# A warm-up of wide and thin matrix products in place of 22 transposes, ahead of a fused attention and MLP kernel

## The chip, the cores and the metric

The kernel runs on one core of a Trainium2 chip. The metric is device time in microseconds (us). Beside the two timed runs there is one profiled execution, whose span (first to last instruction) is 913.8 us.

## The reference

```python
def _A_ref(x, wqkv, wo):                       # x: 1 x 2048 x 640, 32 heads of 20, window of 256
    qkv = (x @ wqkv).reshape(B, S, 3, H, Dh).transpose(2, 0, 3, 1, 4)
    q, k, v = qkv[0], qkv[1], qkv[2]
    scores = einsum("bhqd,bhkd->bhqk", q, k) * Dh ** -0.5
    scores = where(mask, scores, -1e9)         # causal, 256 keys back
    o = einsum("bhqk,bhkd->bhqd", softmax(scores), v)
    return o.transpose(0, 2, 1, 3).reshape(B, S, D) @ wo

def _B_ref(x, w1, b1, w2, b2):                 # 640 -> 1536 -> 640
    h = relu(x @ w1 + b1)
    return (h * h) @ w2 + b2

xn = layernorm(x)
return x + _A_ref(xn, wqkv, wo) * silu(_B_ref(xn, w1, b1, w2, b2))
```

All inputs and the output are fp32. Nothing of the warm-up enters the output.

## The kernel before

Every fp32 matrix is split into a high part rounded to fp32r and a low part, and a product is taken as three fp32r products (high by high, high by low, low by high). The attention's inner products use bf16 and fp16 pieces in the same way.

The first stage normalizes x in four blocks of 512 rows, transposes them on TensorE, and computes q, k (first group of 128 columns) and v. The second stage walks over 16 pairs of heads by 16 blocks of 128 queries, and between its steps a filler feeds TensorE with the remaining q and k groups, the MLP's two layers and at last the output projection.

In the first stage the order of work on all five engines is the order in which the code writes it (`manual_schedule`). It begins like this. ScalarE loads its table (line 275). TensorE runs the warm-up: `WARM` = 22 transposes of an identity matrix into one PSUM tile (line 278), which wait only for GpSimd to make the identity. Meanwhile SyncE issues the loads of the first four tiles of x (`load_x`, line 134) and of the weights for k and q (`load_w`, line 174) and v (line 298). VectorE takes the statistics of x (`stats`, lines 142 and 143), ScalarE the root (line 302), VectorE the reciprocal and the normalized rows `xn` (lines 305 and 151). TensorE transposes `xn` in five pieces of 128x128 (line 311), runs ten more transposes of the identity (line 325, `WARM2`), and goes on with the next tile. ScalarE and VectorE take the high and low parts out of PSUM (lines 317 and 321). The first products of q and k are at line 200, those of v at line 230. Line 578 is the helper through which most wide products of the second stage go, line 527 the product of the attention's weights with v (61 columns), lines 448 and 492 the scores, lines 464, 465 and 474 a row of maxima that is transposed on TensorE.

The pools: `bigp` has eight buffers of 128 x 2560 four-byte elements, used for x transposed and large weights; `pat` has two PSUM buffers under each of the tags "s" and "st"; `pmm` has three.

The lines of the warm-up:

```python
warm_ps = pmm.tile([P, P], F32, tag="mm", name="warm_ps")
for _ in range(WARM):
    nc.tensor.transpose(warm_ps, ident, ident)
```

Of the kernel before, what the change touches and what calls it, by code (L numbers as in the profile page):

```python
# [7 lines left out]
F32 = mybir.dt.float32  # L8
F32R = mybir.dt.float32r
BF16 = mybir.dt.bfloat16  # L10
# [4 lines left out]
P = 128  # L15
# [23 lines left out]
WARM = 22  # L39
# [12 lines left out]
def attn_mlp_kernel(ctx: ExitStack, tc, x, wqkv, wo, w1, b1, w2, b2, out):  # L52
    nc = tc.nc
    PSUM = bass.MemoryType.PSUM
    const = ctx.enter_context(tc.tile_pool(name="const", bufs=1))
    bigp = ctx.enter_context(tc.tile_pool(name="bigp", bufs=8))
    pmm = ctx.enter_context(tc.tile_pool(name="pmm", bufs=3, space=PSUM))
    pat = ctx.enter_context(tc.tile_pool(name="pat", bufs=2, space=PSUM))
# [21 lines left out]
    ident = const.tile([P, P], F32, name="ident")  # L80
# [46 lines left out]
    with tc.tile_pool(name="ph1v", bufs=2) as p1v, tc.tile_pool(name="ph1", bufs=2) as p1, tc.tile_pool(name="ph1x", bufs=4) as p1b, tc.tile_pool(name="ph1w", bufs=1) as p1w:  # L127
# [145 lines left out]
        with tc.manual_schedule(engines={E_.PE, E_.Activation, E_.DVE, E_.Pool, E_.SP}):  # L273
            warm = p1.tile([P, 1], F32, tag="warm", name="warm")
            nc.scalar.activation(warm, eps, AF.Sqrt)
            warm_ps = pmm.tile([P, P], F32, tag="mm", name="warm_ps")
            for _ in range(WARM):
                nc.tensor.transpose(warm_ps, ident, ident)
            ws0, ws1 = {}, {}
            load_x(0, 3)  # L280
            raws = [load_w(group_src(0, "k"), KC)]
# [159 lines left out]
    def scores(p, q, between):  # L441
        i = p % 2
        k0 = max(0, q - 2)
        nk = (q - k0 + 1) * P
        r = []
        for hh in range(2):
            ps = pat.tile([P, 4 * P], F32, tag="s", name="sps")
            nc.tensor.matmul(ps[:, :nk], qs[i][0:KR, hh, q * P:(q + 1) * P], ks[i][0:KR, hh, k0 * P:k0 * P + nk], start=True, stop=True)  # L448
            r.append(ps)
            if not hh:  # L450
                rows = between and between(ps)
        return (r, nk), rows
# [547 lines left out]
    with tc.manual_schedule(engines={E_.PE, E_.Activation, E_.DVE, E_.Pool, E_.SP}):  # L1000
# [6 lines left out]
        for s in range(steps):  # L1007
# [17 lines left out]
            rows = between = None  # L1025
            if s % 4 == 0 and 0 < s <= NP * NT:
                def between(tp=None, s=s):
                    return max_rows((s - 1) // NT, (s - 1) % NT // 4, tp)
            if a:
                sc, rows = scores(p, q, between)  # L1030
            elif between:
                rows = between()
# [58 lines left out]
```

## Time and profile before

| what | value |
|---|---|
| time, median of two runs | 915.86 us (915.09 to 916.62) |
| span of the profiled execution | 913.8 us |
| TensorE products, busy | 893.6 us, 98% |
| TensorE weight loads, busy | 746.9 us, 82% |
| VectorE, busy | 759.1 us, 83% |
| ScalarE, busy | 668.6 us, 73% |
| GpSimd, busy | 544.9 us, 60% |
| mean granted TensorE clock | 0.998 |

The profile names engines PE (TensorE products), PEld (its weight loads), DVE (VectorE), ACT (ScalarE), POOL (GpSimd) and SP (SyncE). A timeline row gives the start in us, the time in us from the first start to the last end of the instructions merged into it, the engine, the line of the code, the operation with output and inputs, and how many there are; in brackets stands the idle time before it and what ended it. A row of a group gives busy time and the mean duration of one in ns. The records of a matrix product overlap, since products are pipelined, so a record is longer than the distance from one product to the next.

### The profile page before, as it was taken

To read this page: it belongs to the slowest core of one execution; us is meant where nothing else is said; L and a number is where in the kernel's file an instruction comes from. 1 tells how busy PE (TensorE), PEld (TensorE's weight loads), DVE (VectorE), ACT (ScalarE), POOL (GpSimd) and SP (SyncE) were. 2 spreads that over 40 slices of the span, in tenths; PEclk is the share of its full clock that TensorE was granted. 3 is DMA by queue.
4 is the path that set the end of the run, shared out by engine and by line. 5 is a ranking of instruction groups with operands and counts; after the bars stand their busy time and mean duration, and the time that the engine had idled before them with its cause. 6 is when DMAs were issued, how large, how long until landed. Compare 5 with 4: busy or idle time off the path is not lost.

```text
span 913.8 us, 21792 instructions
## 1 busy us (share of the span) xinstructions
PE 893.6 (98%) x7632; PEld 746.9 (82%) x7632; DVE 759.1 (83%) x2031; ACT 668.6 (73%) x1282; POOL 544.9 (60%) x832
## 2 busy tenths in 40 slices
PE   8999999999999999999999999999999999999998
PEld 8999977776766678788788788778788788789998
DVE  7875478999899998998888999998988988975554
ACT  5454348898889896987886988976986977994321
POOL 6010017797789785886785876775775976772000
PEclk9999999999999999999999999999999999999999
DMA  6899786767777454244264245365174264156873
GB/s 240 279 394 350 219 266 201 233 209 237 250 237 237 142 180 131 89 155 132 67 203 152 69 123 153 103 224 152 51 262 136 75 211 145 27 158 222 286 272 117
DMA packets 130803, 168.79 MB, mean 185 GB/s; under 512 B 44100, under 2 KB 91268, under 8 KB 128132
## 3 DMA queue, kind: packets, MB, share of 16 engines
q1 hardware_dynamic: 130692, 167.39, 56.3%
q8 instruction: 60, 0.98, 0.4%
q14 instruction: 51, 0.42, 0.1%
HBM read 96.15 MB, written 70.91 MB: 183 GB/s over the span
## 4 chain that ended last, share of the span: by engine, by line
PE 73%; DVE 9%; ACT 8%; DMA 4%; issue 3%; POOL 2%; SPq 1%; ACTq 0%; DVEq 0%; POOLq 0%
PE yps L872 14%; PE hps L578 14%; PE wops L578 8%; PE sps L448 7%; PE qkps L578 7%; PE ops L527 7%; PE stps L492 6%; PE vps L230 5%; ACT p L499 3%; DVE junk L460 2%; PE qkps L200 2%; DVE pl L513 2%; ACT ph L507 1%; DMA v_d<-vt 1%; ACT relu L827 1%
## 5 line engine op out<-in xcount | busy, mean ns | idle before, releaser
L499 ACT ACTIVATE p<-stps,ebias 128x384 f32<-128x384 f32 (+2 forms) x512 | 258.7, 558 | 85.2 <-PE stps L492 72.9
L460 DVE CUSTOM_DVE_ANT_0 junk<-sps,mask 128x384 bf16<-128x384 f32 (+2 forms) x512 | 250.5, 525 | 47.3 <-PE sps L448 40.8
L513 DVE TENSOR_TENSOR pl<-p,ph 128x768 f16<-128x768 f32 (+2 forms) x256 | 251.3, 982 | 1.9 <-ACT ph L507 1.9
L500 POOL TENSOR_SCALAR_AFFINE_SELECT p<-p 128x256 f32<-128x256 f32 x256 | 166.9, 652 | 128.4 <-ACT p L499 112.0
L507 ACT ACTIVATE ph<-p 128x768 f16<-128x768 f32 (+2 forms) x256 | 204.6, 799 | 4.1 <-POOL p L502 3.0
L872 PE MATMUL yps<-w,hh 128*128 128x320 f32 x768 | 183.8, 320 | 0.0
L578 PE MATMUL hps<-xb,w 128*128 128x512 f32 x630 | 172.1, 410 | 0.0
L578 PEld LDWEIGHTS hps<-xb,w 128*128 128x128 f32 x630 | 115.3, 188 | 24.1
L872 PEld LDWEIGHTS yps<-w,hh 128*128 128x128 f32 x768 | 130.7, 188 | 5.0 <-issue 0.6
L448 PE MATMUL sps<-ks,qs 120*128 120x384 bf16 (+2 forms) x512 | 128.2, 319 | 4.5 <-DVE mt L460 4.4
L872 PE MATMUL yps<-w,hl 128*128 128x320 f32 x384 | 122.5, 319 | 0.0
L492 PE MATMUL stps<-qs,ks 122*128 122x384 bf16 (+2 forms) x512 | 120.8, 316 | 1.2 <-DMA qs<-mrow 1.0
L502 POOL TENSOR_SCALAR_AFFINE_SELECT p<-p 128x256 f32<-128x256 f32 x224 | 109.0, 487 | 0.0
L527 PEld LDWEIGHTS <-ph 128*128 128x128 f16 x1440 | 85.9, 97 | 25.6 <-issue 20.6
L527 PE MATMUL ops<-vp,ph 128*128 128x61 bf16 x1440 | 100.9, 192 | 0.0
L527 PE MATMUL ops<-vp,pl 128*128 128x61 bf16 x1440 | 99.7, 191 | 0.0
L831 POOL TENSOR_TENSOR hl<-sq,hh 128x256 fp32r<-128x256 f32 x96 | 77.5, 808 | 18.9 <-DVE sq L830 15.6
L527 PEld LDWEIGHTS <-pl 128*128 128x128 f16 x1440 | 87.7, 97 | 0.0
L872 PEld LDWEIGHTS yps<-w,hl 128*128 128x128 f32 x384 | 72.2, 188 | 1.5
L492 PEld LDWEIGHTS <-ks 122*128 122x128 bf16 x512 | 49.0, 98 | 29.5 <-issue 2.5
L230 PE MATMUL vps<-wv,xT 128*128 128x320 f32 x480 | 71.7, 308 | 0.2 <-DVE r L255 0.2
L230 PEld LDWEIGHTS vps<-wv,xT 128*128 128x128 f32 x480 | 70.5, 188 | 0.6 <-DVE r L255 0.5
(116 smaller groups left out, 1480.3 us busy)
## 6 DMA issues: line engine op xcount, KB each, us to landing
ks<-k_d SPq DMA_DIRECT2D x64, 240.0 KB
qs<-q_d SPq DMA_DIRECT2D x64, 240.0 KB
xb<-xs SPq DMA_DIRECT2D x12, 1280.0 KB
xs<-xT SPq DMA_DIRECT2D x8, 1280.0 KB
y<-ysb SPq DMA_DIRECT2D x32, 320.0 KB
q_d<-shm SPq DMA_DIRECT2D x38, 256.0 KB
v_d<-vt SPq DMA_DIRECT2D x8, 976.0 KB
vp<-v_d SPq DMA_DIRECT2D x16, 488.0 KB
```

Source lines behind the costliest of these rows:

```text
L230: nc.tensor.matmul(ps, xT[xp][b][:, c * BT + t * P: c * BT + (t + 1) * P], wv[wp][:, c, nh * HALF:(nh + 1) * HALF], start=first and m == 0 ...
L448: nc.tensor.matmul(ps[:, :nk], qs[i][0:KR, hh, q * P:(q + 1) * P], ks[i][0:KR, hh, k0 * P:k0 * P + nk], start=True, stop=True)
L460: nc.vector.tensor_tensor_reduce(out=junk[:, :nk], in0=r[hh][:, :nk], in1=mask[:, 3 * P - nk:], scale=1.0, scalar=-3.0e38, op0=ALU.add, op ...
L492: nc.tensor.matmul(ps[:, :n], ks[i][0:KR + 2, hh, kb * P:(kb + 1) * P], qs[i][0:KR + 2, hh, kb * P:kb * P + n], start=True, stop=True)
L499: nc.scalar.activation(p32[:, hh, :n], r[hh][:, :n], AF.Exp, scale=SCALE, bias=ebias)
L500: nc.gpsimd.affine_select(p32[:, :, 0:P], p32[:, :, 0:P], pattern=[[0, 2], [1, P]], compare_op=ALU.is_ge, fill=0.0, base=0, channel_multip ...
L502: nc.gpsimd.affine_select(p32[:, :, 2 * P:], p32[:, :, 2 * P:], pattern=[[0, 2], [-1, P]], compare_op=ALU.is_gt, fill=0.0, base=0, channel ...
L507: nc.scalar.activation(ph[:, :, :n], p32[:, :, :n], AF.Copy)
L513: nc.vector.tensor_sub(pl[:, :, :n], p32[:, :, :n], ph[:, :, :n])
L527: nc.tensor.matmul(ot[:, q % 4, hh, :], t[:, hh, (q - k) * P:(q - k + 1) * P], vp[:, k // 4, k % 4, hh, :], start=m == 1, stop=m == 2 * le ...
L578: nc.tensor.matmul(ps, a, b_, start=j == 0, stop=j == n - 1)
L872: nc.tensor.matmul(pss[nh], hs[fc][hp][:, tt * P:(tt + 1) * P], lin1(wt2, (wp * NFH + fc) * D + nh * HALF, HALF), start=fc == 0 and j == 0 ...
```

## The change

The 22 transposes are replaced. Three tiles of 128x512 are taken from `bigp`: one bf16 and one fp32 filled with ones, one fp32r copied from the fp32 one. The results go to four PSUM tiles of the pool `pat` and are never read. `part` issues one product on `rows` rows; where these are fewer than 128, successive products go to successive halves or quarters of the rows. `thin` issues products of 21 columns (or n), with the weights taken from four places in turn; `whole` issues products of 512 columns on all rows. Everything behind the warm-up keeps its order; lines behind it stand 33 lines further down.

```diff
             warm_ps = pmm.tile([P, P], F32, tag="mm", name="warm_ps")
-            for _ in range(WARM):
-                nc.tensor.transpose(warm_ps, ident, ident)
+            wbf = bigp.tile([P, 512], BF16, tag="big", name="wbf")
+            wfr = bigp.tile([P, 512], F32R, tag="big", name="wfr")
+            wfp = bigp.tile([P, 512], F32, tag="big", name="wfp")
+            for w_ in (wbf, wfp):
+                nc.vector.memset(w_, 1.0)
+            nc.vector.tensor_copy(wfr, wfp)
+            wps = [pat.tile([P, 512], F32, tag=t_, name="wps") for t_ in ("s", "s", "st", "st")]
+
+            def part(rows, j, bank, n, t_=wfp, o=0):
+                r0 = rows * (j % (P // rows))
+                nc.tensor.matmul(wps[bank][:, :n], t_[r0:r0 + rows, o:o + P], t_[r0:r0 + rows, :n], start=True, stop=True)
+
+            def thin(rows, count, n=21, t_=wfp):
+                for j in range(count):
+                    part(rows, j, j % (P // rows), n, t_, j % 4 * P)
+
+            def whole(n, t_=wfr):
+                for j in range(n):
+                    part(P, 0, j % 4, 512, t_)
+
+            whole(16, wbf)
+            whole(2)
+            thin(P, 24)
+            whole(2)
+            thin(64, 24)
+            whole(2)
+            thin(32, 24)
+            whole(2)
+            thin(P, 24, 61, wbf)
+            whole(2)
+            for _ in range(6):
+                part(64, 1, 1, 512, wfr)
+                for j in range(4):
+                    part(64, 0, 0, 21, wfp, j * P)
+            whole(2)
             ws0, ws1 = {}, {}
```

## The prediction

> **What bounds the kernel now.** I read the page first (shares of the engines, then the chain that ended last), then the timeline of TensorE's first microseconds, then busy time by stretch.
>
> ```profile
> span 913.8 us, 21792 instructions
> PE 893.6 (98%) x7632; PEld 746.9 (82%) x7632; DVE 759.1 (83%) x2031; ACT 668.6 (73%) x1282; POOL 544.9 (60%) x832
> ...
> PE 73%; DVE 9%; ACT 8%; DMA 4%; issue 3%; POOL 2%; SPq 1%; ACTq 0%; DVEq 0%; POOLq 0%
> ```
>
> TensorE is busy 98% of the span and carries 73% of the chain. What is put in front of its work therefore has little slack to fall into. The change sits at the very front, so the question is when TensorE turns to its first real work, the transposes of x at line 311.
>
> ```profile
> 0.80 0.21 POOL L81 MEMSET ident<- 128x128 f32 x1 [0.29 <-POOLq L1078]
> 0.94 0.42 POOL L86 MEMSET mask<- 128x384 f32 x1
> 1.75 4.10 PE L278 MATMUL warm_ps<-ident 128*128 128x128 f32 x22 [1.75 <-POOL ident L82]
> 3.78 0.89 DVE L142 BATCH_NORM_STATS2 st<-xt 128x6 f32<-128x320 f32 x2 [3.78 <-DMA xt<-in_A_x_dram]
> 6.63 0.76 PE L311 MATMUL tps<-ident,xn 128*128 128x128 f32 x5 [0.79 <-DVE xn L151]
> 7.24 1.25 PE L325 MATMUL warm_ps<-ident 128*128 128x128 f32 x10
> 8.33 0.71 PE L311 MATMUL tps<-ident,xn 128*128 128x128 f32 x5
> 8.87 1.26 PE L325 MATMUL warm_ps<-ident 128*128 128x128 f32 x10
> 9.96 0.73 PE L311 MATMUL tps<-ident,xn 128*128 128x128 f32 x5
> 10.45 0.84 PE L200 MATMUL qkps<-xT,wgkh 128*128 128x256 f32 x5
> ```
>
> The old warm-up ends at 1.75 + 4.10 = 5.85. TensorE then waits 0.79 us for the normalized rows (xn) and starts real work at 6.63. From there it hardly stops, as the stretches show (columns: us, then busy us and instructions of PE, PEld, DVE, ACT, POOL, then the granted clock, DMA share and GB/s):
>
> ```profile
> 5.00:10.00 5.00, 4.21 (x39) 3.94 (x38) 4.82 (x15) 2.87 (x8) 0.62 (x1) 1.00 0.97 330
> 10.00:15.00 5.00, 5.00 (x42) 4.69 (x41) 4.29 (x12) 3.99 (x9) 4.34 (x3) 1.00 1.04 413
> 15.00:20.00 5.00, 5.00 (x42) 5.00 (x41) 4.71 (x15) 2.96 (x8) 5.00 (x5) 1.00 0.28 99
> ```
>
> So the old warm-up is free: it lies under the load of x and the statistics, and the first real transpose waits for VectorE. A warm-up that ends after 6.63 delays everything by the excess.
>
> **The change, part by part.** Removed: 22 transposes, 4.10 us, all under the wait for xn. Removing them gains nothing.
>
> Added on VectorE: two fills and one copy of 128x512. VectorE's first record is at 3.78, where it waits for x. A fill of 128x384 took 0.42 us on another engine, so three operations of perhaps 0.4 to 0.6 us end near 2.5 and stay under that wait. Without the cover they would cost at most some 1.5 us. The engines take up work at 0.80 (GpSimd's first row), and TensorE can start once the first fill is done, at about 0.8 + 0.4 = 1.2.
>
> The order and waits of every other engine are unchanged, SP's and GpSimd's queues included. TensorE's order behind the warm-up is unchanged too. Two of the first transposes also wait for the last warm-up product on their PSUM buffer, which lies four transposes back and is done by then.
>
> Added on TensorE: 34 wide products (512 columns: 16 bf16, 12 fp32r on all rows, 6 fp32r on half the rows), 24 bf16 products of 61 columns, and 96 fp32 products of 21 columns (24 on 128 rows, 24 alternating between halves, 24 going round the quarters, 24 more in six groups of four beside the half-row wide ones). The compiled program has 7860 pairs of weight load and product against 7632. That is 7632 - 22 + 58 + 2 x 96, so each fp32 product stands there as two pairs.
>
> Rows for the prices. First the old warm-up up to 3.5 us; then nine wide products from the chain; two weight loads of transposes and two of fp32r products, each pair after an idle stretch; the first and last of 24 bf16 products of 61 columns.
>
> ```profile
> 1.75 1.97 PE L278 MATMUL warm_ps<-ident 128*128 128x128 f32 x8 [1.75 <-POOL ident L82]
> ...
> 125.74 2.06 PE qkps L578 x9
> ...
> 6.63 0.20 PEld L311 LDWEIGHTS tps<-ident,xn 128*128 128x128 f32 x2 [1.02 <-DVE xn L151]
> ...
> 11.27 0.30 PEld L200 LDWEIGHTS qkps<-xT,wgkl 128*128 128x128 f32 x2 [0.20 <-POOL wgkl L179]
> ...
> 295.38 0.20 PE L527 MATMUL ops<-vp,ph 128*128 128x61 bf16 x1
> ...
> 296.05 0.19 PE L527 MATMUL ops<-vp,pl 128*128 128x61 bf16 x1
> ```
>
> ```profile
> L325 PEld LDWEIGHTS warm_ps<-ident 128*128 128x128 f32 x20 | 2.2, 141 | 0.0
> L200 PEld LDWEIGHTS qkps<-xT,wgkl 128*128 128x128 f32 x25 | 4.1, 189 | 0.8 <-POOL wgkl L179 0.2
> L278 PE MATMUL warm_ps<-ident 128*128 128x128 f32 x22 | 4.1, 370 | 1.7 <-POOL ident L82 1.7
> L325 PE MATMUL warm_ps<-ident 128*128 128x128 f32 x20 | 2.5, 272 | 0.0
> ```
>
> - **Clock.** The old transposes begin slowly. Eight take 1.97 us; less the end of the last (about 0.42, the rest of its record) that is 0.22 us apart. Ten at line 325 take 1.25, less 0.27: 0.109 apart. That is half speed, then full. For 22 to take 4.10 us, about 14 must have been slow, some 3.1 us. I take 3.5 us at half speed for the new start.
> - **Wide products.** 2.06 / 9 = 0.229 us each, taken for bf16 too. Sixteen are 3.66 us, plus 1.75 for the half-speed stretch; twelve are 2.75.
> - **Thin bf16.** (296.05 - 295.38) / 23 = 0.029 us each; 24 are 0.7 us.
> - **Thin fp32.** No row has one. 21 columns are a third of the 61 that pass in 0.029 us, so the two weight loads set the time. A transpose's load lasts 0.141 us, and two span 0.20, so they follow at about 0.057. An fp32r load lasts 0.189, two span 0.30: 0.108 apart. In the program, the first load of an fp32 product carries the mode of a transpose's load and the second that of an fp32r load, so I add 0.057 + 0.108 = 0.165 and take 0.175 us per product. Bounds: 0.058 (two pairs at the thin bf16 pace) and 0.218 (two pairs at the pace of transposes, 0.109).
> - **On all rows**: 24 x 0.175 = 4.2 us.
> - **On halves and quarters** loads into different rows may run side by side. Halves lie between 0.085 and 0.175; I take 0.13, so 3.1 us. Quarters lie between 0.058 and 0.175; I take 0.105, so 2.5 us.
> - **Six groups** of four thin products beside a wide one on the other half: 0.70 if the wide one hides, 0.93 if not. I take 0.80, so 4.8 us (4.0 to 6.0).
> - **Changes between row shapes**: no row. Six, from nothing to one product's latency each (0.27): 0 to 1.6, I take 0.3.
>
> Full-speed sum: 1.2 + 3.66 + 1.75 + 2.75 + 4.2 + 3.1 + 2.5 + 0.7 + 4.8 + 0.3 = 25.0. The first real transpose would start at 25.0 instead of 6.63, a delay of 18.4 us. VectorE is ahead by then only up to the point where it needs TensorE's transposes, and TensorE ran without gaps from 6.63, so I count no recovery.
>
> The Trainium skill, "FP8 and Floating Point Precision", section TensorE Precision Notes, says that true FP32 takes four passes through the array; if each pass brought its own load, a thin product would cost about twice my price (a rival below).
>
> **What the clock adds.** Once in the old trace TensorE falls to half speed in mid-run:
>
> ```profile
> 294.90:298.30 3.40, 1.66 (x28) 0.96 (x26) 3.17 (x8) 2.64 (x6) 2.77 (x3) 1.00 0.95 310
> 298.40:301.80 3.40, 3.20 (x10) 2.39 (x11) 3.40 (x10) 2.85 (x6) 3.32 (x5) 0.50 1.02 322
> ```
>
> A stretch of 3.4 us with 1.66 us busy is followed by one at clock 0.50. Of its 28 products 24 are the thin bf16 ones (0.7 us); with the few wide ones columns moved for some 1.3 us, under two fifths. A thin fp32 product moves 21 columns twice: 42 x 0.029 / 61 = 0.02 us of 0.175, an eighth (a quarter if each pair passes its columns twice). The three thin stretches last 4.2, 3.1 and 2.5 us with only 0.46 us of wide products between. If moving columns is what the clock follows, it falls at about 12 us and returns with the wide and bf16 products near the end. Some 12 us at half speed cost 6 us more: first transpose at 31.0, delay 24.4.
>
> The Trainium skill, "TensorE: Matmul & The Clock Gate", Part 1, describes such a gate, with a window of about 3.4 us; the two rows above agree with the length. Its Part 4 says that transposes do not bring the full clock, by which the old warm-up warmed nothing and real matmuls could win time; the rows at lines 278 and 325 (0.22, then 0.109 apart, with nothing but transposes) speak against it here.
>
> **Forecast: slower.** The profiled execution took 913.8 in its span, the median shown is 915.86, so 2.06 lie around the span. 913.8 + 24.4 + 2.06 = 940.3, that is +2.7%. 2% is 18.3 us, about what a measurement of this kernel can tell from no change.
>
> **Rivals.**
> 1. **Full clock, little help from row groups.** For it: TensorE's sequence stays dense, and loads may count as work. Against it: the half-speed window above. Halves and quarters at 0.16 each, the six groups at 0.9: 25.0 + 0.7 + 1.3 + 0.6 = 27.6, delay 21.0, 936.9.
> 2. **Not slower by 2%: loads into different row groups overlap, at full clock.** Place: the 72 products on halves and quarters. At 0.085, 0.058 and 0.66 a group: 25.0 - 1.1 - 1.1 - 0.8 = 22.0; with 0.165 for the product on all rows and free changes 21.4: delay 14.8, 930.7. It decides once the first real transpose comes before 24.9. Against it: both loads of one product go to the same rows. The Trainium skill, "TensorEngine Tiling (Array Packing)", section Key Properties, says that different tiles can load and multiply in parallel; no run here shows it yet.
> 3. **An fp32 product costs four loads.** 4 x 0.109 = 0.436 us, without overlap: 96 x 0.436 = 41.9 in place of 14.6, delay 45.7, 961.6. Against it: two loads per product in the program.
>
> **How the numbers follow.** Forecast 0.55, rival 1 0.15, rival 2 0.25, rival 3 0.05. The low end is rival 2 with a somewhat earlier start (929). The high end: the forecast with serial loads and half speed over all thin products, 27.6 + 10 = 37.6, delay 31, 947, and 3 us for a real start still at half speed: 950. What is left out is rival 3 and a little on each side. Slower by over 2%: 0.54 + 0.15 + 0.05 = 0.74; within 2%: rival 2 and the edge of the forecast, 0.25; faster: 0.01, since nothing is removed that anyone waited for.
>
> **What would show it.** In the profile after: the first record of line 344 (the old 311) at 31, with TensorE busy before it and no idle wait for xn; a granted clock of 0.50 somewhere between 9 and 28 us; thin fp32 pairs on all rows about 0.09 apart on average at full clock; the rest of the span shifted as a block, about 907 us from the first real transpose to the end as now. I would be wrong if the clock stays at 1.00 through the thin stretches, if halves and quarters come at a half and a quarter of the price, or if later stages give back part of the delay.

## The result, and the profile after

The changed kernel took 945.87 us (two runs, 943.19 and 948.54) against 915.86: 1.033 times as long, with a 95% interval of 1.029 to 1.037. The forecast was 940.3, slower. The execution shown below is the one of 948.54.

The page of the kernel after (span; busy time, share and instructions of each engine; granted clock in 40 slices, in tenths; chain that ended last):

```profile
span 946.8 us, 22252 instructions
...
PE 927.5 (98%) x7860; PEld 775.6 (82%) x7860; DVE 763.2 (81%) x2034; ACT 668.5 (71%) x1282; POOL 544.7 (58%) x832
...
PEclk7699999999999999999999999999999999999999
...
PE 79%; DVE 8%; ACT 6%; DMA 4%; issue 2%; SPq 1%; POOL 0%; DVEq 0%; ACTq 0%; POOLq 0%
```

The span grew by 33.0 us and TensorE's busy time by 33.9. Beside TensorE only VectorE's busy time grew, by 4.1, of which 1.4 are the fills and the copy. Only the first two slices of the clock line are below full speed. So the loss should lie at the front, which TensorE's timeline shows (start, time from first start to last end, line, operation, count):

```profile
1.52 5.22 PE L287 MATMUL wps<-wbf 128*128 128x512 bf16 x16 [1.52 <-DVE wbf L281]
...
7.04 6.11 PE L287 MATMUL wps<-wfp 128*128 128x21 f32 x48
12.98 1.20 PE L287 MATMUL wps<-wfr 128*128 128x512 f32 x2
14.11 5.31 PE L287 MATMUL wps<-wfp 64*128 64x21 f32 x48
...
20.50 2.77 PE L287 MATMUL wps<-wfp 32*128 32x21 f32 x48
...
27.72 1.87 PE L287 MATMUL wps<-wfp 64*128 64x21 f32 x8
29.22 0.79 PE L287 MATMUL wps<-wfr 64*128 64x512 f32 x1
29.43 1.87 PE L287 MATMUL wps<-wfp 64*128 64x21 f32 x8
...
38.01 1.27 PE L344 MATMUL tps<-ident,xn 128*128 128x128 f32 x5
...
43.86 0.84 PE L200 MATMUL qkps<-xT,wgkh 128*128 128x256 f32 x5
```

The first real transpose starts at 38.01 instead of 6.63, a delay of 31.4 us. The first product of q and k starts at 43.86 instead of 10.45: 33.4. The rest is shifted as a block; the span grew by 33.0. The extra 2 us between the two marks are explained by the clock (columns: stretch; its length; busy us and count of PE, PEld, DVE, ACT, POOL; clock; DMA share; GB/s):

```profile
8.20:11.60 3.40, 3.40 (x33) 3.40 (x32) 0.23 (x2) 0.00 (x0) 0.00 (x0) 1.00 1.03 402
11.70:15.00 3.30, 3.30 (x19) 2.65 (x19) 0.00 (x0) 0.00 (x0) 0.00 (x0) 0.50 0.60 238
...
21.90:25.20 3.30, 3.30 (x49) 2.73 (x46) 0.00 (x0) 0.00 (x0) 0.00 (x0) 0.50 0.00 0
...
35.60:38.90 3.30, 3.30 (x14) 2.96 (x15) 0.00 (x0) 0.00 (x0) 0.00 (x0) 0.50 0.00 0
39.00:42.30 3.30, 3.30 (x18) 3.30 (x17) 2.53 (x4) 1.57 (x5) 1.54 (x1) 0.50 0.00 0
42.40:45.70 3.30, 3.30 (x31) 3.30 (x30) 3.23 (x9) 2.64 (x7) 0.97 (x1) 1.00 0.35 99
```

The trace's clock records put the half speed at 11.61 to 42.33, which is 30.7 us, nine windows of 3.413 us. TensorE is "busy" in all of them. 26.4 us of it lie ahead of the first real transpose, 4.3 us lie in the real work. The 4.3 cost half, 2.15 us. Half of the 26.4 would be 13.2, which would put the first real transpose at 38.0 - 13.2 = 24.8 at full speed. That is an estimate, and somewhat low, because a thin pair takes 0.213 us at half clock and 0.112 at full (both below), a little less than twice as long. The run e3 below gives a better one. Its thin products cost the same and its clock fell only at 24.96. Its first real transpose stands at 26.40; less 0.72 for the half-speed end, plus 0.15 because its full clock came 0.3 us earlier at the start, that is 25.8. So the half clock cost some 12.2 us ahead of the real work.

The sum of the whole span closes. Before had one window at half speed in mid-run (1.7 us lost); after has one too, at 332.46. 913.8 + 31.4 + 2.15 = 947.3, against 946.8 measured.

The two runs of the kernel after, 5.3 us apart, differ in this too: mean clock 0.982 over 946.8 us is 17.0 us lost, 0.987 over 941.5 is 12.2.

What a thin product costs shows in the same timeline cut off before the clock fell, and in the group of its weight loads:

```profile
7.04 4.65 PE L287 MATMUL wps<-wfp 128*128 128x21 f32 x41
```

```profile
L287 PEld LDWEIGHTS wps<-wfp 128*128 128x128 f32 x36 | 4.1, 192 | 0.0
```

41 pairs span 4.65 us; less the rest of the last record (some 0.17) and by 40 steps that is 0.112 us from pair to pair, 0.224 for a product of two. At half clock the starts in the trace are 0.213 apart. Each load lasts on average as long (192 ns) as that of an fp32r product (189), not as a transpose's (141).

### The profile page after: what moved, and what is told of

Its sections match the earlier page's. It is cut to its first block, busy times and chain, and to the rows that moved or that the text cites. A ratio compares the mean times of both kernels' runs of the same rounds, so it can differ in the third digit from the quotient of the medians.

```text
span 946.8 us, 22252 instructions
## 1 busy us (share of the span) xinstructions
PE 927.5 (98%) x7860; PEld 775.6 (82%) x7860; DVE 763.2 (81%) x2034; ACT 668.5 (71%) x1282; POOL 544.7 (58%) x832
## 4 chain that ended last, share of the span: by engine, by line
PE 79%; DVE 8%; ACT 6%; DMA 4%; issue 2%; SPq 1%; POOL 0%; DVEq 0%; ACTq 0%; POOLq 0%
PE yps L905 16%; PE hps L611 14%; PE wops L611 7%; PE qkps L611 7%; PE ops L560 7%; PE sps L481 7%; PE stps L525 7%; PE vps L230 5%; PE wps L287 4%; DVE junk L493 3%; ACT p L532 2%; PE qkps L200 2%; DVE pl L546 2%; DMA v_d<-vt 1%; ACT ph L540 1%
```

## The experiments

The theory after the result: the clock follows the share of time in which columns move through the array, and 21 columns are too few. The rivals are named with each run. "Before" runs on the same chip beside each group: 914.99 (e1 to e4), 913.95 (f1 to f4), 914.83 (g1 to g4).

### e1: the thin fp32 products left out

```diff
-            thin(P, 24)
             whole(2)
-            thin(64, 24)
             whole(2)
-            thin(32, 24)
...
                 part(64, 1, 1, 512, wfr)
-                for j in range(4):
-                    part(64, 0, 0, 21, wfp, j * P)
```

> The 96 thin fp32 products are left out; the 34 wide ones and the 24 thin bf16 ones stay. Theory: the warm-up delays the real work one for one, and only the thin fp32 products bring the clock down. Then the clock is 1.00 from about 4.8 us on, the first real transpose starts at 1.5 + 4.9 + 18 x 0.229 + 0.7 = 11.2 us, a delay of 4.6 over the kernel before: about 920.5 us. Rival: a few us of delay are absorbed later (DMA is ahead): about 916 us.

Measured: 921.8 us, 1.0075 [1.0056, 1.0095], clock 1.000. Of the 3.3% that the change costs, 2.6 points belong to the thin fp32 products and the half clock that comes with them. The timelines of e1 (TensorE, VectorE and GpSimd) show one thing that nobody had expected:

```profile
11.62 0.71 PE L339 MATMUL tps<-ident,xn 128*128 128x128 f32 x5
...
13.88 1.93 DVE L151 TENSOR_SCALAR xn<-xt,mv,rstd 128x640 f32<-128x640 f32 x1
13.92 1.54 POOL L179 TENSOR_TENSOR wgkl<-raw,wgkh 128x640 fp32r<-128x640 f32 x1 [10.69 <-ACT wgkh L178]
...
15.96 0.74 PE L339 MATMUL tps<-ident,xn 128*128 128x128 f32 x5 [0.90 <-DVE xn L151]
```

The same two operations in the kernel before:

```profile
9.19 0.61 DVE L151 TENSOR_SCALAR xn<-xt,mv,rstd 128x640 f32<-128x640 f32 x1
9.38 1.84 POOL L179 TENSOR_TENSOR wgkl<-raw,wgkh 128x640 fp32r<-128x640 f32 x1 [6.35 <-ACT wgkh L178]
```

The normalization of the third tile takes 1.93 us instead of 0.61, because it now meets GpSimd's subtraction at its start, and TensorE waits 0.90 us for it. Before, GpSimd was the one that took longer (1.84 instead of 1.54). In the kernel after the same meeting stands at 40.72 and 40.76 (1.93 and 1.55), hidden there by TensorE's half clock. The Trainium skill, "SBUF — State Buffer", section Who interferes with whom, says that an operation of this kind (`tensor_scalar`) on VectorE can run in a mode that needs a pair of ports shared with GpSimd, and that the engine that issues first then keeps the pair for its whole instruction while the other is blocked. The 1.93 and the 1.84 agree with that; the trace shows the delay, not the ports. f4, below, moves the subtraction.

### e2 and e3: 128 and 64 columns in place of 21

```diff
-            thin(P, 24)
+            thin(P, 24, 128)
...
-                    part(64, 0, 0, 21, wfp, j * P)
+                    part(64, 0, 0, 128, wfp, j * P)
```

(likewise for the halves and quarters; e3 has 64 in the place of 128)

> The 96 fp32 products move 128 columns instead of 21; loads and row groups stay. Theory (the clock follows the time in which columns move): the clock stays at 1.00, every pair of load and product takes about 0.112 us on all rows, half and a quarter of that on halves and quarters; first real transpose at 6.4 + 2.75 + 5.4 + 2.7 + 1.35 + 0.7 + 5.4 + 0.3 = 25 us, about 934 us. Rival (row groups, fp32 loads or their changes bring the clock down, whatever the columns): clock 0.50 for some 30 us as in the changed kernel, first transpose at 38 or later, 946 us or more.

> The 96 fp32 products move 64 columns instead of 21. Theory that each pair passes its columns twice (128 column times of 0.42 ns in 0.112 us, near one half of the time): the clock stays at 1.00, about 934 us. Rival (each pair passes them once: a quarter of the time): the clock falls to 0.50 in the stretch on all rows as in the changed kernel, about 946 us.

Measured: e2 934.92 us, 1.0217 [1.0194, 1.0241]; e3 933.87, 1.0213 [1.0192, 1.0233]. More work in each product, and the kernel is 11 to 12 us faster than with 21 columns. The timeline of e2's TensorE, and one stretch of its windows:

```profile
8.41 5.52 PE L287 MATMUL wps<-wfp 128*128 128x128 f32 x48
...
14.32 2.95 PE L287 MATMUL wps<-wfp 64*128 64x128 f32 x48
...
17.86 1.62 PE L287 MATMUL wps<-wfp 32*128 32x128 f32 x48
...
27.44 0.71 PE L344 MATMUL tps<-ident,xn 128*128 128x128 f32 x5
```

```profile
7.60:10.90 3.30, 3.30 (x28) 3.06 (x27) 1.45 (x4) 0.00 (x0) 0.00 (x0) 1.00 1.07 399
```

The 48 pairs span 5.52 us, less the rest of the last record (some 0.2) 0.113 apart, as with 21 columns. On halves it is 0.058 (2.95), on quarters 0.030 (1.62), about a half and a quarter. So neither loads nor columns of different row groups wait for each other, and the number of columns up to 128 costs nothing. 912.1 (before without its mid-run window) + 27.44 - 6.63 = 932.9, against a span of 933.0: at full clock the delay is passed on one for one.

e3 tells how often the columns pass. At 0.426 ns per column ((0.229 - 0.120) / 256, the spacings of products of 512 and 256 columns) 64 columns are 27 ns, 24% of the 112 ns of a pair, or 49% if they pass twice. The clock stayed at 1.00 through e3's all-rows, half and quarter stretches. In the kernel before it had fallen after a window (294.96 to 298.37) in which the columns of the products make about 35%: 24 x 0.026, 0.164 for one of 384 columns and 0.40 for two wide ones, the first of which begins before the window, are 1.18 of 3.41 us. So, if one level holds for all products, they pass twice per pair. Weight loads do not seem to count: they fill the stretch ahead of the fall in the kernel after (3.40 of 3.40 us, above). It fell for one window only, which begins in the six groups and holds the first real transpose:

```profile
26.40 1.27 PE L344 MATMUL tps<-ident,xn 128*128 128x128 f32 x5
```

```profile
21.60:24.90 3.30, 3.30 (x36) 3.30 (x34) 0.00 (x0) 0.00 (x0) 0.00 (x0) 1.00 0.00 0
25.00:28.30 3.30, 3.30 (x14) 2.88 (x14) 0.18 (x1) 0.81 (x3) 0.00 (x0) 0.50 0.00 0
```

There columns move for 0.218 + 8 x 0.0545 = 0.65 us of a group's 0.89, which is 73%, but on half of the rows: 37%. That the rows weigh in was the next theory.

### e4: the thin products in short stretches, wide ones between

```diff
-            thin(P, 24)
-            whole(2)
-            thin(64, 24)
-            whole(2)
-            thin(32, 24)
-            whole(2)
+            for rows, count in ((P, 8), (P, 8), (P, 8), (64, 12), (64, 12), (32, 24)):
+                whole(6)
+                thin(rows, count)
+            whole(6)
             thin(P, 24, 61, wbf)
-            whole(2)
             for _ in range(6):
+                whole(2)
                 part(64, 1, 1, 512, wfr)
```

> The same thin products in short stretches (8, 8, 8 on all rows, 12, 12 on halves, 24 on quarters), six wide products ahead of each stretch, two wide ones ahead of each of the six groups: 38 wide products more than the changed kernel. Theory (column time): no window of 3.4 us falls under two fifths, the clock stays at 1.00; pairs 0.112 us on all rows, products 0.112 on halves, 0.056 on quarters; first real transpose near 36 us, in spite of the 38 added products, about 945 us. Rival (thin fp32 products bring the clock down by themselves): 0.50 through most of it, first transpose past 55 us, 965 us or more.

Measured: 952.13 us, 1.0409 [1.0389, 1.0428]. The expectation counts the wide products wrongly: 7906 pairs against 7860 are 46 more. The windows of e4:

```profile
14.90:18.30 3.40, 3.40 (x27) 2.85 (x28) 0.00 (x0) 0.00 (x0) 0.00 (x0) 1.00 0.02 5
...
28.60:31.90 3.30, 3.30 (x25) 2.51 (x24) 0.00 (x0) 0.00 (x0) 0.00 (x0) 1.00 0.00 0
32.00:35.30 3.30, 3.30 (x16) 2.60 (x14) 0.00 (x0) 0.00 (x0) 0.00 (x0) 0.50 0.00 0
```

Half right. With six wide products between them the thin stretches on all rows, halves and quarters ran at full clock (some 46 to 53% of each window, weighed by rows). In the groups it fell: 2 wide products (0.436) and (0.218 + 8 x 0.0179) / 2 = 0.18 make 0.62 of 1.66 us, 37%. Keeping the clock up by filler cost more than the half clock did.

### f1 and f2: wide products on 32 and on 64 rows

```diff
             whole(16, wbf)
-            whole(2)
-            thin(P, 24)
...
+            for j in range(40):
+                part(32, 0, j % 4, 512, wfr)
             whole(2)
```

(f2 has 64 in the place of 32; nothing else of the warm-up is left)

> The warm-up is 16 wide bf16 products, then 40 wide fp32r products on one quarter of the rows (32), then two wide ones on all rows. Columns move nearly all the time, in a quarter of the rows. Theory (the clock follows moving columns weighted by the rows they use, and falls where a window of 3.4 us is under about two fifths): the clock falls to 0.50 near 12 us and stays there until a window is full again; first real transpose near 20 us, about 931 us. Rival (columns count whatever the rows): clock 1.00, first real transpose at 6.4 + 40 x 0.229 + 0.5 = 16.1 us, about 926 us.

> As the run on 32 rows, with the 40 wide products on one half of the rows. Theory (rows weighted: one half, over two fifths): the clock stays at 1.00, first real transpose at 16.1 us, about 926 us. Rival (anything less than all rows counts as idle): it falls as on 32 rows, about 931 us.

Measured: f1 931.41 us, 1.0190 [1.0168, 1.0212]; f2 923.98, 1.0116 [1.0088, 1.0144]; first real transposes at 20.81 and 16.41. One stretch of f1 and the same of f2:

```profile
12.60:15.90 3.30, 3.30 (x10) 2.50 (x9) 0.00 (x0) 0.00 (x0) 0.00 (x0) 0.50 0.40 158
```

```profile
11.40:14.70 3.30, 3.30 (x16) 2.66 (x15) 0.00 (x0) 0.00 (x0) 0.00 (x0) 1.00 0.76 302
```

At full clock columns move for 0.218 of each 0.234 us in both. On 32 rows (93% x 1/4 = 23%) the clock fell, on 64 (47%) it did not. This settles that the rows count. That they count in proportion fits all runs here, and was not tested by itself.

### f3: sixteen wide products in the middle of the half-speed stretch

```diff
             whole(2)
+            whole(16, wbf)
             thin(P, 24, 61, wbf)
```

> The changed kernel with 16 more wide bf16 products behind the stretch on quarters, where the clock is at half. Theory (a fallen clock returns only after a window that is full to about four fifths): it returns near 28.7 us in the midst of the added products, falls once more in the six groups, and the first real transpose starts at about 39 us, no more than 1 to 2 us later than in the changed kernel though 16 wide products are added: 947 us. Rival (it returns on its own after the thin stretches or not before the real work, whatever stands between): the clock stays at 0.50, first real transpose at 38.0 + 16 x 0.427 = 44.8 us, 953 us.

Measured: 948.77 us, 1.0376 [1.0354, 1.0397]; first real transpose at 38.73. The windows of f3:

```profile
24.10:27.40 3.30, 3.30 (x9) 1.19 (x9) 0.00 (x0) 0.00 (x0) 0.00 (x0) 0.50 0.00 0
27.50:30.80 3.30, 3.30 (x39) 1.88 (x36) 0.00 (x0) 0.00 (x0) 0.00 (x0) 1.00 0.02 5
...
34.40:37.70 3.30, 3.30 (x17) 3.27 (x17) 0.00 (x0) 0.00 (x0) 0.00 (x0) 0.50 0.00 0
```

One window full of wide products brought the clock back, and the groups (20% with 21 columns) took it again. An earlier window of f3 narrows the level from above: from 6.99, where the full clock began, to 10.41 columns move for 1.11 us in wide products and for 16% of 2.28 us in thin ones, some 43%, and the clock stayed. In the kernel after, the windows around the wide and bf16 products hold 51 to 60% and did not bring it back. So to return, the clock wants more than to stay.

### f4: e1 with the first split of weights ahead

```diff
+            split_w(*wjobs.pop(0))
             highs(t0_)
...
             rests(t0_)
-            split_w(*wjobs.pop(0))
```

(on top of e1's edit)

> The run without thin fp32 products, with the split of k's weights (ScalarE, then GpSimd) issued while TensorE is still in the warm-up, instead of beside VectorE's third normalization. Theory (about 1 us of that run is VectorE's normalization held up by GpSimd's subtraction, 1.93 us instead of 0.61): the third normalization takes 0.61 us again, TensorE's wait for it is gone, the third set of transposes starts 3.3 us after the first instead of 4.3, and the time falls by 1 us to about 920.8 us. Rival (the long normalization has another cause): it stays at 1.9 us and the time at 921.8 us.

Measured: 920.52 us, 1.0064 [1.0044, 1.0085]. Its timeline at the place of the collision:

```profile
12.39 0.71 PE L339 MATMUL tps<-ident,xn 128*128 128x128 f32 x5
...
14.65 0.61 DVE L151 TENSOR_SCALAR xn<-xt,mv,rstd 128x640 f32<-128x640 f32 x1
...
15.66 0.71 PE L339 MATMUL tps<-ident,xn 128*128 128x128 f32 x5
```

The normalization takes 0.61 us again, and the third transposes follow the first by 3.27 us instead of e1's 4.34. That meeting the split causes the 1.93 is shown; its ScalarE part moved along, but ends before the 1.93 begins, so it is the subtraction. That it is worth a microsecond of the whole time is not: 1.0064 and 1.0075 can't be told apart, and the first transpose came 0.77 us later here.

### g1 and g2: a short warm-up, and none

```diff
-            whole(16, wbf)
-            whole(2)
-            thin(P, 24)
...
+            whole(12, wbf)
```

```diff
-            for _ in range(WARM):
-                nc.tensor.transpose(warm_ps, ident, ident)
```

(g1 changes the kernel after, g2 the kernel before)

> The warm-up is 12 wide bf16 products alone. Theory (a warm-up that ends before the normalized rows of x are there costs nothing, whatever it consists of): they end at 1.5 + 12 x 0.427 = 6.6 us at the latest, the first real transpose starts at about 6.7 us, and the time is that of the kernel before, about 915 us. Rival (wide products warm the clock where transposes do not): the real work runs faster than in the kernel before, 912 us or less.

> The 22 transposes are left out and nothing stands in their place; the two groups of ten between the first real transposes stay. Theory (the clock needs a full window of work first): the first real transpose starts at 6.6 us as before, but at half clock until about 8 to 12 us, which costs 1 to 2.5 us: 916 to 917.5 us. Rival (the warm-up does nothing): 915 us, and the first real transposes are 0.109 us apart from the start.

Measured: g1 913.88 us, 0.9986 [0.997, 1.0002]; g2 917.93, 1.0037 [1.0016, 1.0057]. TensorE's timeline in g1, then in g2:

```profile
1.52 4.59 PE L287 MATMUL wps<-wbf 128*128 128x512 bf16 x12 [1.52 <-DVE wbf L281]
6.68 0.74 PE L330 MATMUL tps<-ident,xn 128*128 128x128 f32 x5 [0.57 <-DVE rstd L324]
```

```profile
6.70 1.30 PE L309 MATMUL tps<-ident,xn 128*128 128x128 f32 x5 [6.70 <-DVE rstd L303]
7.80 2.34 PE L323 MATMUL warm_ps<-ident 128*128 128x128 f32 x10
9.93 1.13 PE L309 MATMUL tps<-ident,xn 128*128 128x128 f32 x5
10.89 1.25 PE L323 MATMUL warm_ps<-ident 128*128 128x128 f32 x10
...
12.45 0.84 PE L200 MATMUL qkps<-xT,wgkh 128*128 128x256 f32 x5
```

Twelve wide products end in time and leave everything where it was: no gain over the transposes. Without any warm-up the first transposes come 0.213 us apart, and from 10.78 on, after one window of nothing but transposes, 0.109. The first product of q and k is 2.0 us late (12.45 against 10.45). The Trainium skill, "TensorE: Matmul & The Clock Gate", Part 4, says that transposes do not bring the full clock; here they did.

### g4: short fp32r products against fp32 ones

```diff
             whole(2)
-            thin(P, 24)
+            thin(P, 24, 22, wfr)
             whole(2)
...
+            thin(P, 12)
             whole(2)
```

> Price by itself: behind 16 wide bf16 and 2 wide fp32r products stand 24 fp32r products of 22 columns on all rows, 2 wide ones, 12 fp32 products of 21 columns on all rows, 2 wide ones. Theory (a weight load of 128 columns of four-byte data takes 0.11 us whatever the mode, and an fp32 product has two): the fp32r products follow at 0.112 us, the fp32 ones at 0.224. Rival (the second of the fp32 product's pairs, or its second pass over the columns, sets the price): the fp32r products follow at less than 0.08 us. First real transpose at 6.4 + 0.65 + 2.7 + 0.64 + 2.7 + 0.64 = 13.7 us, about 923 to 925 us.

Measured: 924.88 us, 1.0121 [1.0095, 1.0148]; first real transpose at 18.02. TensorE's windows:

```profile
7.40:10.70 3.30, 3.30 (x28) 3.05 (x26) 1.17 (x4) 0.00 (x0) 0.00 (x0) 1.00 1.06 392
10.80:14.10 3.30, 3.30 (x16) 3.11 (x15) 0.00 (x0) 0.00 (x0) 0.00 (x0) 0.50 0.97 383
```

The starts of the fp32r products of 22 columns are 0.112 us apart in the trace until the clock falls at 10.76: the price of one weight load, the same as for a pair of the fp32 ones. Those of 21 columns ran at half clock here, 0.213 per pair (12.05 to 17.02, 24 pairs). The price is as expected; the fall was not foreseen, though 9 of each 112 ns say that it must come: the window ahead of it holds some 33%, with weight loads in 3.05 of its 3.30 us. The first transpose is 4.3 us later than expected. About 1.3 is the full clock coming late at the start in this execution (the first wide fp32r product stands at 7.66, in the kernel after at 6.39). The half clock from 10.76 to 18.02 costs some 3.5 more, so that without both it would have come about 0.5 earlier than expected. The expected time was met by the median of the four runs all the same. This execution is the slowest of them (927.66; the others are 922.55 to 925.5), so run and place are not to be set against each other closely.

## Why the prediction came out as it did

- **Place and direction: right.** The old warm-up was free, the new one ends after 6.63 and is passed on. g1 shows both: the same kernel with a warm-up that ends in time takes the old time. VectorE's fills and copy stayed hidden, as counted: the first is done at 1.46, and VectorE still waits for x, until 3.91, when the third ends at 2.47.
- **Full-speed sum: 25.0 against some 25.8, near by luck, since its errors cancel.** The thin product on all rows was put at 0.175 and is 0.224, since the first of its two loads is as dear as the second, whatever mode it carries. Halves were put at 0.13 and are 0.112; quarters at 0.105 and are 0.056: exactly a half and a quarter of the price on all rows. The groups were put at 0.80 and are 0.89, the eight pairs on their half alone, with the wide product hidden. Changes between stretches cost more than the 0.05 put down for each: two wide products between two stretches take 0.64 instead of 0.46. Only a part of that is the change of rows, because in e4 six wide products take 0.1 too long between stretches on all rows (1.49 and 1.45 instead of 1.37), and 0.2 where rows change (1.58 to 1.60). That halves and quarters come at a half and a quarter of the price is one of the signs by which the prediction said it would be wrong, and on that point it was.
- **The clock: right mechanism, wrong size; this is the step that failed.** It fell at 11.61 (12 was said) for the reason given. But it was to come back "with the wide and bf16 products near the end"; it stayed down to 42.33. The term of 6 us measured some 12.2 ahead of the first real transpose and 2.15 behind it. The step took one level for falling and returning. The runs show two. The clock stayed at 43% (f3) and at 46 to 49% (e3, e4, f2), and fell at 16 to 37% (after, before, f1, g4, the groups of e3 and e4). It returned after windows of 78% or more, not after 51 to 60% (after), and not after 76%. The last two figures come from the start: in e1 the clock returned at 4.19, 2.67 us after the first product, which is 78% of a window; in e2 the first window ended at 4.12, 2.60 us after it, and the full clock came one window later, at 7.53.
- **The columns pass twice per pair** (by e3, as said there), which the prediction left open (an eighth or a quarter of the time). 21 columns make 2 x 9 / 112 = 16%, and the rows do not change that, because on quarters four times as many pairs pass on a quarter of the rows.
- **No recovery: right**, 947.3 by the sum against 946.8. The collision of VectorE and GpSimd was not foreseen. It costs TensorE 0.90 us of waiting in e1, and in the kernel after nothing that the trace shows.
- **Rivals.** Rival 2's mechanism was true (row groups do overlap, as the Trainium skill, "TensorEngine Tiling (Array Packing)", section Key Properties, says of different tiles; halves at 0.112 and quarters at 0.056 agree), its full clock was not. e2 is that rival's condition made real, first real transpose 27.44. Rival 1's full clock fell with the row of 0.50, rival 3's four loads with the spacing of 0.112.
- **Open:** the exact levels, between 37 and 43% and between 76 and 78%; the shares are counted from the starts of the products, good to a per cent or two. That a transpose's columns pass twice (2 x 128 x 0.426 = 0.109, its spacing) is worked out, not shown by a run of its own.

## What to carry to other kernels

A warm-up is free only up to the moment when the first real input is ready; here 12 wide products or 22 transposes fill that time, and nothing was gained by the wide ones. A TensorE that the profile calls 100% busy can still lose its clock: what counted here was columns moved, weighed by rows, so products of 21 columns on all rows let it fall, on halves and quarters they did not raise it again, and it took a window more than three quarters full to bring it back. When an added stretch is priced, the clock is to be reckoned window by window, to its end and into the real work.

## What the hardware showed beyond expectation

- Each of the two pairs of an fp32 product cost the same 0.112 us with 21, 64 and 128 columns, and so did an fp32r product of 22: up to there the load sets the time. e2 with six times the columns was 1.2% faster than the kernel after, because the clock stayed up.
- Products on different halves or quarters of the rows ran side by side without loss: 0.112 and 0.056 us per fp32 product at full clock (e2, e4), twice that at half clock (the kernel after).
- The clock's windows do not start with the kernel. The same first products got the full clock at 4.19 in e1, at 4.78 in the kernel after and at 7.53 in e2.
- A VectorE operation of 0.61 us took 1.93 when it started together with a GpSimd subtraction, although its record starts 0.04 us earlier than GpSimd's.
